# First attention chunks of a three-stage kernel: values pooled on TensorE, softmax by half tiles, reordered loads, and products of zeros

## The chip, the cores and the metric

The kernel runs on one core of a Trainium2 chip. The metric is device time in microseconds, the median of several runs. One execution was profiled; it has its own time and a span (first to last instruction).

## The reference

Three stages, one after the other, all in float32:

```
k_p, v_p = mean of k, v over groups of 8 rows                  # (4 batches, 8 heads, 576 rows, 64) -> 72 rows
attn = softmax(q @ k_p.T / 8) @ v_p                            # -> x: 2304 tokens x 512
x = (relu(x @ w_in) ** 2) @ w_out                              # 512 -> 2048 -> 512
e = argmax(x @ w_gate); g = its softmax probability            # 8 experts, capacity 576
out[i] = g[i] * (relu(x[i] @ w1[e]) @ w2[e])                   # 512 -> 1024 -> 512, if the expert has room
```

## The kernel before, in words

The 2304 tokens are nine chunks of 256 (`NCH`), a chunk two token tiles of up to 128 (`tiles_of_chunk`). Each chunk runs through attention, then through the dense layer in 16 slices of 128 hidden units (`g1`: the product `h`, relu, square, a split into a high and a low part, and the second product into `y`). Chunks 0 and 1 share the time in which the dense layer's weights arrive and are split, so their slices alternate; chunks 2 to 8 follow one by one, each with the next chunk's attention between its slices. Routing and the experts follow.

*Precision.* The large products run in float32r, a form with a shorter mantissa, one record of the trace a product. So every operand is split into a high and a low part, and a product is three: high by high, low by high, high by low. The products of attention (`qk` L429, the values L556) are plain float32. `conv` (L266) loads one of 32 dense weight tiles (128 x 512) and makes the two parts: `last` and `scale` on ScalarE, `sign` and `merge` on VectorE, `high` on ScalarE, `low` on VectorE (L307).

*Attention of one token tile.* `k_pool` (L328) sums groups of 8 columns of a head pair's keys on VectorE, `k_place` (L373) copies the sums into `kT` so that two heads of a pair share a product. `v_pool` (L347) sums the values likewise, in five blocks of 128 rows, and `v_zero` (L388) multiplies each block with masks into `vz` on GpSimd. `a_scores` (L418) loads a query tile, makes the scores of heads 0 to 3 and of heads 4 to 7 in two products each (the half-tiles `a` = 0 and 1), then the maximum, the subtraction, the exponential, the sum, its inverse, and the normalisation (`norm` L469, on GpSimd, or on VectorE for the tiles in `NORM_DVE`). In chunks 0 to 2 (`DVE_SOFTMAX`) the subtraction is one VectorE instruction for four heads and the exponential one on ScalarE; elsewhere ScalarE makes it head by head with the sum (L447). The sum, its inverse and the normalisation wait for all eight heads. `a_trans` (L511) transposes the probabilities in five blocks and ScalarE copies them out; `a_values` (L540) multiplies them with `vz` and splits the result into `xh` and `xl`, which the dense layer reads.

*What sets the order.* Every step is handed to a planner (`Steps`, L113) by `add(priority, engine, cost, function, reads, writes)`. It plays the program with costs in nanoseconds: at each turn it takes, over all engines, the step that can start first, by priority within an engine (lower is earlier), and emits it. Its clocks are only a plan; what it fixes is the order in each engine's queue, and the engines run their queues in order. It doubles the cost of TensorE's steps until TensorE has been busy for a while, and lengthens VectorE's steps marked `port` that meet a GpSimd step (`SHARE`). The constants ahead of the code (L62 to L82) are priorities: `CH0` and `CH1` place the attention of chunks 0 and 1, `Q0` their query loads, `V0_LOAD` and `CONV_LOAD` the loads of values and of weight tiles, `CONV_LEAD` and `CONV_AHEAD` how far ahead of its use a tile is split and loaded. All these loads are issued by one queue, SP's, in order of priority. `SQUARE_ACT` names the priorities between which chunks 0 and 1 are squared on ScalarE and not on VectorE; a slice's priority is twice its place in the order of slices.

Of the kernel before, what the change touches and what calls it, by code (L numbers as in the profile page):

```python
# [7 lines left out]
F32 = mybir.dt.float32  # L8
# [62 lines left out]
ATT2 = 16  # L71
# [12 lines left out]

def f(ap):
    return ap.bitcast(F32)
# [26 lines left out]
class Steps:  # L113
# [16 lines left out]

    def add(self, prio, eng, cost, fn, r=(), w=(), u=(), lat=0, port=False):
# [36 lines left out]
    def run(self):  # L168
# [6 lines left out]
        while any(todo.values()):  # L175
# [30 lines left out]
            if s.port:  # L206
                o = {"DVE": "POOL", "POOL": "DVE"}[e]
                if self.port[o] > t:
                    cost += min(cost, self.port[o] - t) * self.SHARE[e]
                self.port[e] = t + cost  # L210
# [7 lines left out]
def tile_kernel(ctx: ExitStack, tc: tile.TileContext, q, k, v, w_in, w_out, w_gate, w1, w2, cap, gate_rows, consts, out):  # L218
# [47 lines left out]
    def conv(i, prio, load_prio):  # L266
# [39 lines left out]
        def low():  # L306
            nc.vector.tensor_tensor(out=W[i][:, 1], in0=f(box["a"]), in1=f(W[i][:, 0]), op=ALU.subtract)  # L307

# [3 lines left out]
        add(prio, "ACT", 572, scale, w=(raw,))  # L312
        add(prio, "DVE", 340, sign, r=(raw,), w=(cv,), port=True)
        add(prio, "DVE", 605, merge, r=(raw,), w=(cv,), port=True)
        add(prio, "ACT", 525, high, r=(cv,), w=(("W", i, 0),), u=(whole,))
        add(prio, "DVE", 605, low, r=(cv, ("W", i, 0)), w=(("W", i, 1),), port=True)

# [10 lines left out]
    def k_pool(b, x, prio, load_prio, tag=None):  # L328

        buf, box = Buf("kvraw" if tag is None else tag), {}  # L330

        def load():
            box["raw"] = raw_tile(tag, f"kraw_{b}_{x}")
            nc.sync.dma_start(out=box["raw"], in_=k[b, x])

        def pool():
            nc.vector.tensor_reduce(
                out=kd[:, x], in_=box["raw"].rearrange("p (s r) -> p s r", r=POOL), axis=AX.X, op=ALU.add
            )

        add(load_prio, "SP", 960, load, w=(buf,), lat=2100)
        add(prio, "DVE", 663, pool, r=(buf, "ap"), w=(("kd", x),))

# [3 lines left out]
    def v_pool(b, i, prio, load_prio, tag=None):  # L347
# [20 lines left out]
        if ("v", b, i) in FOLD:  # L368
            add(prio, "POOL", 1300, fold, r=("ap",), w=(buf, ("v", i)))
        else:  # L370
            add(prio, "DVE", 603, pool, r=(buf, "ap"), w=(("v", i),))

    def k_place(b, prio):  # L373
# [44 lines left out]
    def a_scores(c, j, prio, qprio):  # L418
# [67 lines left out]
        for part in [tags] if c == 2 else [tags[:1], tags[1:]]:  # L486
            add(prio(2), "PE", 480 * len(part), lambda part=part: [qk(*x) for x in part],
                r=(qT, *(y for x in part for y in (("kT", 0, x[0]), ("kT", 1, x[0]), ("kT in", x[0]))), "ap", *after),
                w=[cells[x[0]] for x in part], u=us[part[0][0]])
        if c in DVE_SOFTMAX and (c, j) not in ACT_SOFTMAX:  # L490
            for a in range(2):
# [14 lines left out]
        if (c, j) in NORM_DVE:  # L506
            add(prio(4), "DVE", 663, lambda: norm(nc.vector), r=((mxb, 2),), w=((ex, 0), (ex, 1)), u=(mxb, ex), port=True)
        else:
            add(prio(4), "POOL", 1110, lambda: norm(nc.gpsimd), r=((mxb, 2),), w=((ex, 0), (ex, 1)), u=(mxb, ex))
# [620 lines left out]
    def wgb_load():  # L1130
# [7 lines left out]
        st["wgb"] = wgb  # L1138

    add(-100, "DVE", 600, start_up, w=[("kT", a, g) for a in range(2) for g in range(2)])  # L1140
    for x in range(NPAIR):
        k_pool(0, x, -90 + x, -99, f"W{27 + x}" if x < 2 else f"W{11 + x}")
        if x == 1:
            add(-98, "SP", 300, lambda: cst_load(0, C_TRI), w=("cst",), lat=2000)
# [3 lines left out]
    for i in range(5):  # L1148
        v_pool(0, i, V0_AT, V0_LOAD[i], f"W{22 + i}")
    for c, (at0, gap, slope) in enumerate((CH0, CH1)):  # L1150
# [5 lines left out]
        for j in range(2):  # L1156
            a_scores(c, j, lambda x, j=j: place0(x, j), Q0[c, j])
        if c == 0:
            v_zero(0, V0_AT + 1)
# [6 lines left out]
    add(2, "POOL", 100, late, w=("zt",))  # L1166
    add(4, "SP", 300, late_loads, w=("wg4", "capi"), lat=2000)
# [12 lines left out]
    for c in range(NCH):  # L1180
# [7 lines left out]
        if 2 <= c < NCH - 2:  # L1188
            for x in range(16):
                add(done + 1 + x, "DVE", 725, lambda c=c, x=x: logit(c, x % 2, x // 2), r=(lr[x % 2], "wgb", "wp"),  # L1190
                    w=(("lg", c, x),), u=(ysb[c], lgb[c]), port=True)
            late_routing.append((c, done + 18))
        for i in range(2):
            if c == BACK[i][0]:
                for t in range(2):
                    at, buf = place[c, 0] + BACK[i][1] + 8 * BACK[i][2] * t, Buf("kvraw")
                    add(at - 6, "SP", 760, lambda i=i, t=t: y_back(i, t), r=(("yd", i, t), "ap"), w=(buf,), lat=2000)
                    for x in range(8):
                        add(at + BACK[i][2] * x, "DVE", 725, lambda i=i, t=t, x=x: logit(i, t, x), r=(buf, "wgb", "wp", "ap"),
                            w=(("lg", i, 2 * x + t),), u=(lgb[i],), port=True)  # L1200
                late_routing.append((i, at + 8))
# [541 lines left out]
def _columns(q, k, v):  # L1743
# [6 lines left out]
    kt = k.reshape(B, NPAIR, P // D, S, D).transpose(0, 1, 2, 4, 3).reshape(B, NPAIR, P, S)  # L1750
    vt = v.reshape(B, NROW, POOL, D).transpose(0, 1, 3, 2).reshape(B, NROW, D * POOL)
    return np.concatenate(tiles), kt, vt

# [38 lines left out]
```

## Time and profile before

| | |
|---|---|
| median of 3 runs (lowest, highest) | 685.24 us (684.99, 685.41) |
| the profiled execution | 685.61 us, its span 683.9 us |
| TensorE busy | 659.2 us, 96% |
| VectorE, ScalarE, GpSimd busy | 421.9, 326.6, 186.8 us |
| keys and values of batch 0, queries of two chunks | 4 x 288 KB, 4 x 256 + 128 KB, 4 x 256 KB |
| dense weights | 32 x 512 KB |

How to read it: PE is TensorE, PEld its loading of the stationary operand, DVE VectorE, ACT ScalarE, POOL GpSimd, SP the engine that issues loads. A product in plain float32 leaves two records (passes), one in float32r or a transpose one. The length of one product holds its way through the pipeline, so products that follow each other overlap; the distance of their starts is what one costs. Idle time is put down to what ended it last.

### The profile page before, as it was taken

Reading aid. Unit: us, or ns where it says so; the run is one execution under the profiler, and the core shown is the slowest. Engines: PE = TensorE matmul, PEld = TensorE weight load, DVE = VectorE, ACT = ScalarE, POOL = GpSimd, SP = SyncE. Lnnn points to the kernel's source line nnn. Section 1 sums busy time; section 2 is a strip of 40 time slices with the busy share of each in tenths; the row PEclk is TensorE's granted clock in tenths of the full one; section 3 lists DMA queues with packets and bytes.
Section 4 is the critical chain, followed back from the end, with each engine's and each line's share of the span. In section 5 each row is a group of like instructions: output and inputs, shape, how many; then the busy total and the mean of one; then the engine's idle time right before and its main releaser. Section 6 shows DMA issues by size and latency. Waiting matters only on the chain. (4 is left out here: it accounts for less than half of the span.)

```text
span 683.9 us, 11883 instructions
## 1 busy us (share of the span) xinstructions
PE 659.2 (96%) x4211; PEld 593.4 (87%) x4212; DVE 421.9 (62%) x1123; ACT 326.6 (48%) x905; POOL 186.8 (27%) x221
## 2 busy tenths in 40 slices
PE   3799999999999999999999999999999999999996
PEld 2788899999899999989899899998997979889985
DVE  6999997221288999374288647445354556464352
ACT  5898884344353344255344344343432555454352
POOL 1334543223234233234233132242202211301110
PEclk9899999999999999999999999999999999999999
DMA  8998904110222320011010000062005764655110
GB/s 308 395 365 306 296 31 128 58 47 17 92 78 59 93 78 9 1 41 30 1 48 17 2 32 1 2 222 88 1 33 161 246 220 135 209 163 174 48 60 3
DMA packets 40970, 73.46 MB, mean 107 GB/s; under 512 B 8449, under 2 KB 17921, under 8 KB 40768
## 3 DMA queue, kind: packets, MB, share of 16 engines
q1 hardware_dynamic: 38496, 64.89, 28.0%
q0 software_dynamic: 2400, 7.66, 3.4%
q8 instruction: 37, 0.61, 0.4%
q14 instruction: 37, 0.30, 0.1%
HBM read 59.63 MB, written 13.12 MB: 106 GB/s over the span
## 5 line engine op out<-in xcount | busy, mean ns | idle before, releaser
L628 PE MATMUL h<-xh,W 128*128 128x256 f32 x1152 | 213.4, 284 | 0.2
L648 POOL TENSOR_TENSOR gl<-r,gh 128x256 fp32r<-128x256 f32 x144 | 116.9, 812 | 285.1 <-ACT gh L644 184.9
L628 PEld LDWEIGHTS h<-xh,W 128*128 128x128 f32 x1152 | 184.0, 189 | 10.2 <-ACT xh L562 0.3
L661 PE MATMUL y<-W,gh 128*128 128x512 f32 x576 | 185.1, 402 | 0.3 <-DVE W L307 0.3
L628 PE MATMUL h<-xl,W 128*128 128x256 f32 x576 | 161.8, 281 | 0.8 <-DVE xl L566 0.8
L640 DVE SCALAR_TENSOR_TENSOR r<-h,r 128x256 f32<-128x256 f32 x141 | 59.0, 419 | 100.4 <-ACT r L633 100.1
L633 ACT ACTIVATE r<-h 128x256 f32<-128x256 f32 x144 | 55.1, 382 | 123.8 <-PE h L628 104.9
L661 PE MATMUL y<-W,gl 128*128 128x512 f32 x288 | 113.6, 394 | 0.0
L661 PEld LDWEIGHTS y<-W,gh 128*128 128x128 f32 x576 | 99.4, 189 | 15.7 <-DVE W L307 0.6
L628 PEld LDWEIGHTS h<-xl,W 128*128 128x128 f32 x576 | 108.9, 189 | 1.1 <-DVE xl L566 1.0
L644 ACT CAST gh<-r 128x256 fp32r<-128x256 f32 x144 | 58.5, 406 | 77.4 <-DVE r L640 77.0
L1356 PE MATMUL hp<-yh,W 128*128 128x256 f32 (+1 forms) x384 | 74.5, 291 | 0.9 <-issue 0.9
L718 DVE SCALAR_TENSOR_TENSOR junk<-ysb,wgb 128x512 bf16<-128x512 f32 x80 | 68.5, 856 | 1.4
L661 PEld LDWEIGHTS y<-W,gl 128*128 128x128 f32 x288 | 54.1, 188 | 13.1 <-POOL gl L648 0.3
L1356 PEld LDWEIGHTS hp<-yh,W 128*128 128x128 f32 x384 | 61.1, 188 | 1.6 <-issue 1.0
L1325 PE MATMUL po<-W,xh_e 128*128 128x512 f32 x192 | 61.3, 401 | 0.0
L1356 PE MATMUL hp<-yl,W 128*128 128x256 f32 (+1 forms) x192 | 55.7, 290 | 0.0
L250 DVE TENSOR_TENSOR W<-stg,W 128x512 fp32r<-128x512 f32 x64 | 42.3, 689 | 12.4 <-ACT W L249 11.2
L1325 PEld LDWEIGHTS po<-W,xh_e 128*128 128x128 f32 x192 | 34.7, 188 | 6.8
L1362 DVE SCALAR_TENSOR_TENSOR xl_e<-hp,xh_e 128x256 fp32r<-128x256 f32 x48 | 20.2, 422 | 31.4 <-ACT xh_e L1361 31.2
L1314 POOL DMA_INDIRECT out_dram<-ysb,sidx x12 | 11.9, 995 | 98.3 <-ACT ysb L1303 84.7
L471 POOL TENSOR_TENSOR ex<-ex,sm 128x576 f32<-128x576 f32 (+1 forms) x19 | 25.4, 1338 | 47.7 <-DVE sm L467 28.5
(207 smaller groups left out, 908.8 us busy)
## 6 DMA issues: line engine op xcount, KB each, us to landing
stg<-in_moe_w_dram SPq DMA_DIRECT2D x40, 512.0 KB, 5.0
raw<-in_moe_w_in_dram SPq DMA_DIRECT2D x16, 512.0 KB, 7.5
raw<-in_moe_w_out_dram SPq DMA_DIRECT2D x16, 512.0 KB, 7.3
kraw<-in_k_dram SPq DMA_DIRECT2D x16, 288.0 KB, 3.0
out_dram<-zt SPq DMA_DIRECT2D x18, 256.0 KB, 3.6
y_dram<-ysb SPq DMA_DIRECT2D x18, 256.0 KB, 2.1
qT<-in_q_dram SPq DMA_DIRECT2D x16, 256.0 KB, 3.0
vraw<-in_v_dram SPq DMA_DIRECT2D x16, 256.0 KB, 3.6
```

Source lines behind the costliest of these rows:

```text
L250: eng.tensor_tensor(out=lo, in0=src, in1=f(hi), op=ALU.subtract)
L471: eng.tensor_tensor(out=ex[:n], in0=ex[:n], in1=sm[:n].unsqueeze(2).to_broadcast([n, H, SP]), op=ALU.mult)
L628: nc.tensor.matmul(ps, wt[kk][:, l, o:o + P], r[:, kk, :], start=(n == 0), stop=(n == 3 * KD - 1))
L633: nc.scalar.activation(out=box["r"], in_=box["ps"], func=AF.Relu)
L640: nc.vector.scalar_tensor_tensor(out=r, in0=box["ps"], scalar=0.0, in1=r, op0=ALU.max, op1=ALU.mult)
L644: nc.scalar.copy(out=box["gh"], in_=box["r"])
L648: nc.gpsimd.tensor_tensor(out=box["gl"], in0=box["r"], in1=f(box["gh"]), op=ALU.subtract)
L661: nc.tensor.matmul(st["y", c][t], l[:, ts], r, start=(ff == 0 and n == 0), stop=(ff == NF - 1 and n == 2))
L718: nc.vector.scalar_tensor_tensor(out=junk, in0=st["yb", c, t] if c < 2 else st["ysb", c][t], scalar=1.0, in1=st["wgb"][:, e], op0=ALU.mult ...
L1325: nc.tensor.matmul(ps, l, r, start=(fi == 0 and x == 0), stop=(fi == 7 and x == 2))
L1356: nc.tensor.matmul(ps, ww[:, l, o], r[:, kk, 0:n2], start=(kk == 0 and x == 0), stop=(kk == KD - 1 and x == 2))
L1362: nc.vector.scalar_tensor_tensor(out=lo, in0=p_, scalar=0.0, in1=f(h), op0=ALU.max, op1=ALU.subtract)
```

## The change

1. *Products of zeros.* `warm_up(m)` issues m products of the zero tile `zt` by itself (128 x 128, plain float32) into a PSUM tile that nobody reads. 26 of them stand first in TensorE's queue, 13 behind the first half-tile's scores of chunk 0, 2 behind the first half-tile's scores of its second token tile. The zero tile is set at the start.
2. *Values of batch 0 pooled on TensorE.* Eight products with the identity, one for each of the 8 rows of a group, are added up in PSUM (`v_pool0`); VectorE multiplies the result with the masks into `vz`. The rows are laid out by the host so that five blocks take three loads.
3. *Softmax of chunk 0 by halves of four heads* (`HALVES`): sum, inverse and normalisation are made for each half-tile. For the halves in `ACT_HALF` (both of the first token tile; its entries for chunk 1 have no effect) ScalarE makes the exponential head by head with its sum. The second token tile's halves are normalised on VectorE, the first one's on GpSimd.
4. *Order of loads.* The second key tile, the first, the first query tile, the other two key tiles, the second query tile; then values, constants and weight tiles, the fourth weight tile behind the third query tile.
5. *Other engines.* The third key tile of batch 0 is pooled on GpSimd by three additions (`KFOLD`); the low parts of weight tiles 0, 2 and 3 are made on GpSimd (`LOW_POOL`); the squares of ten more slices go to ScalarE.
6. *Constants and planner costs.* Due times, the costs of shared ports, the loads of batch 3, and the last chunk's softmax (`DVE_SOFTMAX`, 8).

```diff
-V0_LOAD = (-70, -70, -70, -70, -70)
-CONV_LOAD = (-96, -96, -95, -95)
-CONV0 = (-20, -19, -18, -17)
+V0_LOAD = (-96.0, -96.4, -94.4)
+K0_LOAD = (-98.6, -99, -98.4, -98.4)
+CST1 = -96.2
+WARM = 26
+CONV_LOAD = (-96, -96, -95, -56.5)
+CONV0 = (-37.8, -19, -18, -17)
...
-CONV_LEAD = 3
-CONV_AHEAD = 6
+CONV_LEAD = 2.4
+CONV_AHEAD = 1.9
...
-CH1 = (0, 2, 0.5)
-V0_AT = -45
-Q0 = {(0, 0): -98.5, (0, 1): -97, (1, 0): -50, (1, 1): -50}
+CH1 = (0, 2, 0.42)
+V0_AT = -45.9
+Q0 = {(0, 0): -98.5, (0, 1): -98, (1, 0): -83.5, (1, 1): -50}
...
-SQUARE_ACT = (-99, 6)
-NORM_DVE = ((0, 1),)
-KV_AT = {1: (20, 1.0), 2: (66, 3), 3: (130, 3)}
-DVE_SOFTMAX = (0, 1, 2)
+SQUARE_ACT = (-99, 26.0)
+NORM_DVE = ((0, 1, 0), (0, 1, 1))
+HALVES = (0,)
+FILL = ((0, 0, 0, 13), (0, 1, 0, 2))
+KFOLD = (2,)
+ACT_HALF = ((1, 1, 1), (0, 0, 1), (1, 0, 1), (0, 0, 0), (1, 1, 0))
+LOW_POOL = (3, 0, 2)
+KV_AT = {1: (20, 1.0), 2: (66, 3), 3: (128.9, 3.93)}
+DVE_SOFTMAX = (0, 1, 2, 8)
...
-    SHARE = {"DVE": 0.7, "POOL": 0.5}
+    SHARE = {"DVE": 1.0, "POOL": 0.4}
...
+        def fold():
+            y = box["raw"].rearrange("p (s r) -> p s r", r=POOL)
+            for w in (4, 2):
+                nc.gpsimd.tensor_tensor(out=y[:, :, 0:w], in0=y[:, :, 0:w], in1=y[:, :, w:2 * w], op=ALU.add)
+            nc.gpsimd.tensor_tensor(out=kd[:, x], in0=y[:, :, 0], in1=y[:, :, 1], op=ALU.add)
...
+    def v_pool0(i, prio, buf):
...
+            for r in range(POOL):
+                nc.tensor.matmul(
+                    o, ident[ps], st["vraw", i][:, :, r], start=(r == 0), stop=(r == POOL - 1)
+                )
...
+            nc.vector.tensor_tensor(out=o, in0=box["ps"][ps].unsqueeze(1).to_broadcast([n, w, D]), in1=m, op=ALU.mult)
...
+        add(prio, "PE", 860, pool, r=(buf, "cst"), w=(h,))
+        add(prio, "DVE", 65 + 69 * w, place, r=(h, "cst", "ap"), w=(("vz", i),))
...
+            for y in FILL:
+                if y[:3] == (c, j, part[0][0]):
+                    add(prio(2), "PE", 108 * y[3], lambda m=y[3]: warm_up(m), r=(cells[y[2]],), w=(warm,), u=us[y[2]])
+        if c in HALVES:
+            for a in range(2):
...
+                add(prio(3), "DVE", 368, lambda a=a: top(a), r=w, w=((mxb, a),), u=(*u, mxb, ex))
+                if (c, j, a) in ACT_HALF:
+                    for h in range(4 * a, 4 * a + 4):
+                        add(prio(3), "ACT", 300, lambda h=h: exp(h), r=w, w=((ex, a), (mxb, a)), u=(*u, mxb, ex))
+                else:
+                    add(prio(3), "DVE", 365, lambda a=a: less(a), r=(*w, (mxb, a)), w=((ex, a),), u=(*u, mxb, ex))
+                    add(prio(3), "ACT", 335, lambda a=a: exp4(a), w=((ex, a),), u=(ex,))
+                    add(prio(4), "DVE", 365, total, r=((ex, a),), w=((mxb, a),), u=(mxb, ex))
+                add(prio(4), "DVE", 220, inverse, w=((mxb, a),), u=(mxb,))
+                if (c, j, a) in NORM_DVE:
+                    add(prio(4), "DVE", 365, lambda norm2=norm2: norm2(nc.vector), r=((mxb, a),), w=((ex, a),), u=(mxb, ex), port=1)
+                else:
+                    add(prio(4), "POOL", 590, lambda norm2=norm2: norm2(nc.gpsimd), r=((mxb, a),), w=((ex, a),), u=(mxb, ex))
+            return
...
+    def warm_up(m):
+        if "warm" not in st:
+            st["warm"] = pg.tile([P, P], F32, tag="g", name="warm")
+        for _ in range(m):
+            nc.tensor.matmul(st["warm"], st["zt"], st["zt"], start=True, stop=True)
...
+    add(-100, "POOL", 300, late, w=("zt",))
+    add(-100, "PE", 108 * WARM, lambda: warm_up(WARM), r=("zt",), w=(warm,))
```

## Rows read from the trace of the kernel before

**Rows 1.** Busy time by stretch: window, length, each engine, PEclk, DMA share, GB/s.

```profile
8.21:26.81 18.60, 12.38 (x59) 11.29 (x59) 17.07 (x34) 13.86 (x31) 4.79 (x6) 0.82 1.04 375
...
26.81:34.46 7.65, 6.65 (x51) 5.97 (x50) 7.65 (x18) 7.35 (x20) 1.85 (x2) 1.00 1.04 410
...
34.46:40.00 5.54, 4.62 (x25) 3.42 (x24) 5.54 (x9) 4.01 (x11) 2.61 (x3) 1.00 1.03 411
...
40.00:640.00 600.00, 597.64 (x3855) 539.19 (x3854) 368.43 (x1016) 282.61 (x809) 172.71 (x200) 1.00 0.29 96
```

**Rows 2.** Who waited for whom, TensorE, whole run: us in total, times, longest.

```profile
PE ata L520 <- DVE ex L471: 3.3, 1, 3.3
...
PE ata L520 <- POOL ex L471: 2.9, 1, 2.9
...
PE sc L432 <- DVE xl L566: 0.5, 1, 0.5
...
PE y L661 <- DVE W L307: 0.3, 1, 0.3
```

**Rows 3.** Busy time by stretch, finer; PEclk is the granted clock.

```profile
19.59:22.30 2.71, 2.71 (x11) 2.62 (x12) 2.65 (x6) 1.33 (x3) 1.52 (x3) 0.50 1.07 395
...
22.30:26.81 4.51, 4.51 (x28) 4.12 (x27) 4.51 (x11) 4.33 (x9) 0.00 (x0) 1.00 1.06 390
```

**Rows 4.** TensorE's timeline: start us, length us, line, operation, tiles, passes.

```profile
8.21 4.08 PE L432 MATMUL sc<-kT,qT 128*128 128x144 f32 x16 [8.21 <-DVE kd L337]
...
25.43 1.63 PE L432 MATMUL sc<-kT,qT 128*128 128x144 f32 x12
...
34.46 0.60 PE L520 MATMUL ata<-cst,ex 128*128 128x128 f32 x4
...
34.90 0.27 PE L525 MATMUL atb<-cst,ex 128*128 128x128 f32 x1
...
39.69 3.72 PE L556 MATMUL av<-aT,vz 128*128 128x256 f32 x16 [0.59 <-ACT aT L530]
...
46.05 0.40 PE L628 MATMUL h<-xh,W 128*128 128x256 f32 x2
...
46.40 0.40 PE L628 MATMUL h<-xh,W 128*128 128x256 f32 x2
```

**Rows 5.** Groups of TensorE instructions by form, whole run: count, busy us, mean ns.

```profile
L556 PE MATMUL av<-aT,vz 128*128 128x128 f32 x32 | 3.9, 275 | 0.0
...
L556 PE MATMUL av<-aT,vz 128*128 128x64 f32 x32 | 3.8, 271 | 0.0
...
L748 PE MATMUL lp<-wg,ytl 128*128 128x8 f32 x32 | 3.7, 251 | 0.0
```

**Rows 6.** Timeline of the first 8 us.

```profile
0.92 0.20 POOL L1117 MEMSET zt<- 128x128 f32 x1
...
6.11 0.75 DVE L337 TENSOR_REDUCE kd<-kraw 128x72 f32<-128x576 f32 x1 [0.93 <-DMA kraw<-in_k_dram]
...
7.44 0.75 DVE L337 TENSOR_REDUCE kd<-kraw 128x72 f32<-128x576 f32 x1 [0.58 <-DMA kraw<-in_k_dram]
```

**Rows 7.** Groups by line, whole run: count, busy us, mean ns, idle before.

```profile
L640 DVE SCALAR_TENSOR_TENSOR r<-h,r 128x256 f32<-128x256 f32 x141 | 59.0, 419 | 100.4 <-ACT r L633 100.1
...
L447 ACT ACTIVATE ex<-sc,mx 128x72 f32<-128x72 f32 (+1 forms) x104 | 32.2, 322 | 7.1 <-DVE mx L442 7.1
...
L447 ACT ACTIVATION_READ_ACCUMULATOR ex<-sc,mx 128x1 f32 (+1 forms) x104 | 21.5, 206 | 0.0
...
L359 DVE TENSOR_REDUCE pv<-vraw 128x64 f32<-128x512 f32 (+1 forms) x20 | 13.4, 674 | 6.1 <-DMA vraw<-in_v_dram 6.1
```

**Rows 8.** Timeline around 76 us: VectorE's low part, TensorE's products.

```profile
76.01 0.69 DVE L307 TENSOR_TENSOR W<-cv,W 128x512 fp32r<-128x512 f32 x1
...
76.51 0.28 PE L628 MATMUL h<-xh,W 128*128 128x256 f32 x1
```

**Rows 9.** Timeline: GpSimd and VectorE side by side, and a merge alone.

```profile
13.98 1.14 POOL L471 TENSOR_TENSOR ex<-ex,sm 128x576 f32<-128x576 f32 x1 [12.86 <-DVE sm L467]
...
14.13 1.54 DVE L298 SCALAR_TENSOR_TENSOR cv<-raw,cv 128x512 int32<-128x512 int32 x1
...
24.79 0.68 DVE L298 SCALAR_TENSOR_TENSOR cv<-raw,cv 128x512 int32<-128x512 int32 x1
```

More of the change, by code (lines that the diff above doesn't have):

```diff
@@ L129, in __init__, with add @@
         self.steps, self.writer, self.readers = [], {}, {}
-    def add(self, prio, eng, cost, fn, r=(), w=(), u=(), lat=0, port=False):
+    def add(self, prio, eng, cost, fn, r=(), w=(), u=(), lat=0, port=0):
         s = Step(prio, eng, cost, fn, lat, port or eng == "POOL")
@@ L208, in run @@
                 if self.port[o] > t:
-                    cost += min(cost, self.port[o] - t) * self.SHARE[e]
+                    cost += min(cost * s.port, self.port[o] - t) * self.SHARE[e]
                 self.port[e] = t + cost
@@ L306, in low @@
         def low():
-            nc.vector.tensor_tensor(out=W[i][:, 1], in0=f(box["a"]), in1=f(W[i][:, 0]), op=ALU.subtract)
+            eng = nc.gpsimd if i in LOW_POOL else nc.vector
+            eng.tensor_tensor(out=W[i][:, 1], in0=f(box["a"]), in1=f(W[i][:, 0]), op=ALU.subtract)
         whole = Buf(f"W{i}")
@@ L312, in conv @@
         add(prio, "ACT", 572, scale, w=(raw,))
-        add(prio, "DVE", 340, sign, r=(raw,), w=(cv,), port=True)
-        add(prio, "DVE", 605, merge, r=(raw,), w=(cv,), port=True)
+        add(prio, "DVE", 340, sign, r=(raw,), w=(cv,), port=2)
+        add(prio, "DVE", 605, merge, r=(raw,), w=(cv,), port=1)
         add(prio, "ACT", 525, high, r=(cv,), w=(("W", i, 0),), u=(whole,))
-        add(prio, "DVE", 605, low, r=(cv, ("W", i, 0)), w=(("W", i, 1),), port=True)
+        add(prio, *(("POOL", 1050) if i in LOW_POOL else ("DVE", 605)), low, r=(cv, ("W", i, 0)), w=(("W", i, 1),), port=1)
     kT = ap.tile([P, NROW], F32, tag="kT", name="kT")
@@ L341, in k_pool @@
         add(load_prio, "SP", 960, load, w=(buf,), lat=2100)
-        add(prio, "DVE", 663, pool, r=(buf, "ap"), w=(("kd", x),))
+        def fold():
[3 more added lines that the diff above has]
+            nc.gpsimd.tensor_tensor(out=kd[:, x], in0=y[:, :, 0], in1=y[:, :, 1], op=ALU.add)
+        if b == 0 and x in KFOLD:
+            add(prio, "POOL", 1450, fold, r=("ap",), w=(buf, ("kd", x)))
+        else:
+            add(prio, "DVE", 663, pool, r=(buf, "ap"), w=(("kd", x),))
     def v_rows(i):
@@ L371, in v_pool, with v_load0, load, pool @@
             add(prio, "DVE", 603, pool, r=(buf, "ap"), w=(("v", i),))
+    def v_load0(i, load_prio, tag):
+        buf = Buf(tag)
+        def load():
+            m = 2 if i < 4 else 1
+            t = cpool.tile([P, 2, POOL * D], F32, tag=tag, name=f"vraw_0_{i}")
+            if m == 2:
+                src = v[0, 0:4 * P].rearrange("(p i) d -> p i d", i=4)[:, i:i + 2]
+                nc.sync.dma_start(out=t, in_=src)
+            else:
+                nc.sync.dma_start(out=t[v_rows(4), 0], in_=v[0, 4 * P:NROW])
+            for x in range(m):
+                st["vraw", i + x] = t[v_rows(i + x), x].rearrange("p (d r) -> p d r", r=POOL)
+        add(load_prio, "SP", 1300 if i < 4 else 430, load, w=(buf,), lat=2100)
+        return buf
+    def v_pool0(i, prio, buf):
+        ps, n, h, box = v_rows(i), min(P, NROW - i * P), Buf("h"), {}
+        c0, w = max(0, 2 * i - 1), 2 if i in (0, 4) else 4
+        def pool():
+            o = box["ps"] = pp.tile([P, D], F32, tag="h", name=f"pv0_{i}", bufs=2)
+            for r in range(POOL):
+                nc.tensor.matmul(
+                    o, ident[ps], st["vraw", i][:, :, r], start=(r == 0), stop=(r == POOL - 1)
+                )
+        def place():
+            o = vz[ps, c0:c0 + w // 2].rearrange("p s r d -> p (s r) d")
+            m = cst[ps, C_VM + 2 * c0:C_VM + 2 * c0 + w].unsqueeze(2).to_broadcast([n, w, D])
+            nc.vector.tensor_tensor(out=o, in0=box["ps"][ps].unsqueeze(1).to_broadcast([n, w, D]), in1=m, op=ALU.mult)
+        add(prio, "PE", 860, pool, r=(buf, "cst"), w=(h,))
+        add(prio, "DVE", 65 + 69 * w, place, r=(h, "cst", "ap"), w=(("vz", i),))
     def k_place(b, prio):
@@ L506, in a_scores @@
         if (c, j) in NORM_DVE:
[L507 removed]
+            add(prio(4), "DVE", 663, lambda: norm(nc.vector), r=((mxb, 2),), w=((ex, 0), (ex, 1)), u=(mxb, ex), port=1)
         else:
@@ L1147, in tile_kernel @@
     k_place(0, -60)
-    for i in range(5):
-        v_pool(0, i, V0_AT, V0_LOAD[i], f"W{22 + i}")
+    for i in (0, 2, 4):
+        buf = v_load0(i, V0_LOAD[i // 2], f"W{22 + i}")
+        for x in range(i, min(i + 2, 5)):
+            v_pool0(x, V0_AT + 0.1 * x, buf)
     for c, (at0, gap, slope) in enumerate((CH0, CH1)):
```

28 lines of the change are left out of this document (19 added, 9 removed).

## The prediction

> **What bounds the kernel now.** I read the stretches first. From 40 to 640 us TensorE is busy 597.64 of 600.00 us [rows 1]: there the time is the sum of TensorE's work, and a faster helper engine buys nothing. All that can be won lies ahead of 40 us. TensorE does nothing until 8.21 us, is busy 12.38 of the next 18.60, then 6.65 of 7.65 and 4.62 of 5.54 [rows 1]. The list of TensorE's waits names the holes: 2.9 and 3.3 us for the normalised softmax of the two token tiles, later 0.5 us for the second chunk's low part and 0.3 us for a converted weight tile [rows 2]; one of 0.59 for the transposed probabilities stands in the row at 39.69 [rows 4]. The granted clock is at its lower level (0.50, 1.2 GHz) from 19.59 to 22.30 us, when TensorE had just come out of its long waits, and full (1.00, 2.4 GHz) afterwards [rows 3]. At the very start no row shows the clock, but the instructions do: 16 score passes took 4.08 us at 8.21 and 12 took 1.63 us at 25.43, so 255 against 136 ns each [rows 4].
>
> So I make the sum on TensorE, between its first score product (8.21 us) and the end of the fourth group of first-layer products (34.46 us, where transposes start, [rows 4]). At full clock that stretch holds 16 score passes x 0.136 = 2.2, 10 transposes x 0.11 (four from 34.46 to 34.90) = 1.1, 16 value passes x 0.2325 (3.72/16, [rows 4]) = 3.7, the second chunk's 16 score passes 2.2, and 48 first-layer products x 0.1175 (three from 46.05 to 46.40, [rows 4]) = 5.6, where they took 7.65: 14.8 us of work in 26.25 us. At most 11.4 us can be won there, 0.9 more before 40 us [rows 1], and 0.5 after it.
>
> **The change, part by part.** *Zero products at the start.* 26 calls of 128 by 128 in plain float32. The eight score calls ahead of 12.3 us left 16 passes [rows 4], so a call is two passes: 52. They start when the zero tile is set, about 1.1 us (its memset ends there, [rows 6]). A slow pass is 128/144 of the slow score pass, 0.227. After the restart at 19.59 the clock was full 2.7 us later [rows 3]; at 8.21 all 4.08 us of scores ran slow [rows 4]. With a rise 4.1 us after 1.1, 18 passes are slow and 34 x 0.116 (below) follow: the last ends at 9.1; with 2.7 us, at 8.4. I take 8.7. The price per pass is bounded from above by 0.136 (the score row) and from below by 0.110 (the transposes).
>
> *Queries between the keys.* The third load lands near 6.1 (the third key reduction starts there, [rows 6]); with the first query there, the first half's scores could start at about 6.1 instead of 8.21. But TensorE's queue is in order and the zero products stand ahead: they start at 8.7. Half a microsecond is lost, none gained; what is gained is the clock (2.2 against 4.1 us for the scores), and it is counted in the 14.8.
>
> *Zero products between the scores.* 13 calls behind the first half, 2 behind the third: 30 passes x 0.116 = 3.5 us. Queued behind the 13 are the remaining three half-tiles of scores, and behind these VectorE's maxima. The second half's keys are ready at about 9.6 (third key by GpSimd, fourth, now the fifth load, by VectorE up to about 8.9, as an estimate half a microsecond behind its 7.44 + 0.75 now, [rows 6], then the copy that places it), the 13 calls end at 12.3: they overrun the hole that they fill by 2.7 us.
>
> *Values pooled on TensorE.* 5 blocks x 8 calls x 2 passes = 80 passes of 64 columns. The price is the crux. By columns alone a 64-column pass would be half of a transposed 128 columns, 55 ns, 4.4 us in all. But float32 passes here do not get cheaper with fewer columns: 32 of 128 columns took 3.9 us, 32 of 64 took 3.8, 32 of 8 columns took 3.7 [rows 5], that is 0.122, 0.119, 0.116. I take 0.116: 9.3 us (a block of 16 passes 1.86 us, where the planner's cost is 0.86). The nearest row decides, and the form is the same.
>
> The Trainium skill ("TensorE: Matmul & The Clock Gate", section "Back-to-back issue gap") gives 64 columns and fewer about 60 cycles when a product is looked at by itself; by that estimate (25 ns, or 50 if float32 doubles it) the 80 passes would cost 2 to 4 us and the sum below would end faster than before. That is R1's pooled block. The 8-column row contradicts it; the measurement decides.
>
> The five reductions leave VectorE (5 x 0.674 = 3.4 us, [rows 7]), the masked copies move from GpSimd to VectorE (five; no row shows them there, between nothing and the 3.4 us that they replace). All of that lies beside TensorE's longer work and is worth nothing. *Softmax by halves:* the first tile's exponentials go per head to ScalarE (8 x 0.322, or 0.53 with the read of the sum, [rows 7]), VectorE loses two subtractions and a sum and gains reciprocals (no row for a half; I take a wash). It lets a tile's first half be normalised earlier, but transposes wait for both halves. *Moved to other engines:* one key reduction (0.75 us) and the low parts of weight tiles 0, 2, 3 to GpSimd, ten squares (0.42 us on VectorE, [rows 7]) from VectorE to ScalarE. ScalarE is at 7.35 of 7.65 us in that stretch [rows 1]; cover: TensorE's lag gives it 2 us. *Loads:* values (1.15 MB, 3.1 us at the 375 GB/s of [rows 1]) go ahead of the first weight tiles, the fourth weight tile behind a query; weights land about 3 us later, which a TensorE that needs them only after 30 us does not feel. *New costs and due times* reorder everything later, and the last chunk's softmax moves to VectorE: cost 0, covered by the 600 us at 597.64, of which they could take back at most 0.5; if that cover fails, the price is a hole of 0.3 to 0.9 like those in [rows 2].
>
> *Sum.* Start 8.7; work 14.8 + 3.5 + 9.3 = 27.6; end at 36.3 if TensorE never waits, against 34.46: +1.8. Not all waits go: last transposes to copy to values (0.6 us as at 39.69), last pooled block to masked copy to second half of values (0.5, an estimate from the 0.6), and starts and ends of streams. I take +1.3 (bounds 0.5 and 2.5). Given back later: with the helpers ahead, the 0.9 us before 40 us and part of 0.5, together 1.1 (bounds 0 and 1.4). So +2.0 us on the profiled execution's 685.61 (span 683.9): 687.6. That execution is 0.37 above the median of the three runs, so **687.2**. With the pass at 0.110 and the best bounds the sum is -0.3 us, with 0.122 and the worst +5.3.
>
> **Rivals.** *R1, the passes cost what the planner's numbers say* (0.108 a zero call, 0.86 a pooled block): the zero products end at 6.1, then 14.8 + 1.6 + 4.3 = 20.7, end at 26.8 plus 1.3, 6.4 us earlier than 34.46; then VectorE (7.65 of 7.65) and ScalarE bind, each of which must deliver weight tiles earlier too: the twentieth tile is ready at 76.7 when its products start at 76.51 [rows 8], so there is no lead to spend. I take 2.4 back: -4, 681.2. For it: the fillers fit the holes by these costs. Against: [rows 5]. If only the zero calls are cheap, the gain is about 2 (683.3), counted here.
>
> *R2, no difference:* pass at 0.110 (8.8 + 3.3), waits 0.5, 1.4 given back: 8.5 + 26.9 + 0.5 = 35.9, +1.4 - 1.4 = 0: 685.2. For it: the holes are really there to be filled. Against: they are long only where dependent work stands.
>
> *R3, worse: GpSimd holds VectorE up.* A merge took 1.54 us beside a GpSimd product of 1.14 instead of 0.68 [rows 9], +0.86. Three low parts, one key fold and two half normalisations make six such chances, 5.2 us against 2.8 us taken off VectorE (3 x 0.69 by the low part in [rows 8], and 0.75). It decides once VectorE is later than TensorE by the first group of products: 2.4 us more, 689.6. Against: in the same stretch GpSimd loses its masked copies. The Trainium skill ("SBUF — State Buffer", section "Who interferes with whom") calls this an exclusive lock between GpSimd and a VectorE instruction with two SBUF inputs; [rows 9] agree.
>
> **How the numbers follow.** Chances: forecast 0.44, with its own range 685.7 to 689.0; R1 0.31; R2 0.16; R3 0.09. About 0.2% (1.37 us) is what a measurement can tell: faster is below 683.87, slower above 686.61. Faster: R1 0.29 and 0.03 of R2, 0.32. Within: 0.11 of the forecast, 0.12 of R2, 0.02 of R1, 0.25. Slower: 0.33 + 0.09 + 0.01, 0.43. The range leaves out the better part of R1 (0.12) and the far end of R3 and the sum (0.06): 681.0 to 690.0.
>
> **What would show it.** Right: two records per zero call, the last zero product ending near 8.7; pooled passes 0.11 to 0.12 apart; TensorE nearly without waits from 8.7 on and the first first-layer product after 29 us (26.81 now). Wrong: pooled blocks under 1 us, the first scores at about 6.1, the first first-layer product ahead of 25 us; or VectorE, not TensorE, still without a hole at 20 us. That the lower clock vanishes between 15 and 22 us is expected under every case but would fail if the products of zeros did not raise it; then the stretch is slower still.

## The result, and the profile after

The changed kernel takes 689.61 us (median of five runs, 688.86 to 689.89), the kernel before beside it 685.41 us: a ratio of 1.0059, 95% interval 1.0044 to 1.0073. It is slower by 4.2 us where the forecast said 2.0, that is slower as said and by twice as much. The profiled execution took 689.89 us with a span of 688.1 (before: 685.61 and 683.9), so the spans differ by the same 4.2. In the experiments below a time is the median of all runs, and the ratio leaves out runs more than 1.5% above the kernel's fastest.

The page's busy times, after: engine, us, share of the span, instructions.

```profile
PE 676.4 (98%) x4373; PEld 611.3 (89%) x4374; DVE 418.0 (61%) x1120; ACT 327.1 (48%) x899; POOL 188.9 (27%) x223
```

The shortest account stands in that line. TensorE was busy 659.2 us before: it now does 17.2 us more, and stands still 11.7 us of the span instead of 24.7. What was gained in waits, 13.0, was bought with more work than it was worth.

The stretches of TensorE's work after (window, length, each engine's busy time, granted clock, DMA share, GB/s), to be laid beside [rows 1]:

```profile
9.69:31.30 21.61, 21.61 (x171) 20.89 (x169) 15.01 (x38) 13.55 (x39) 3.30 (x4) 1.00 1.04 386
31.30:34.46 3.16, 1.70 (x13) 1.28 (x11) 3.16 (x6) 3.10 (x8) 1.83 (x2) 1.00 1.03 414
34.46:40.00 5.54, 5.34 (x43) 5.13 (x43) 5.53 (x16) 5.54 (x17) 3.23 (x4) 1.00 0.16 66
40.00:640.00 600.00, 596.84 (x3846) 538.05 (x3847) 372.68 (x1017) 285.19 (x800) 173.47 (x201) 1.00 0.30 99
```

From the first score product to the first first-layer product there is not one hole on TensorE and no low clock, where [rows 1] had 12.38 of 18.60 us and [rows 3] a clock of 0.50. VectorE has become the engine with gaps (15.01 of 21.61). But then TensorE, now late and dense, meets helpers that are not ready: 1.70 of 3.16 us.

TensorE's timeline after (start, length, line, operation, tiles, passes, the wait before it), which answers to [rows 4]; the second part is the first-layer products that wait.

```profile
1.04 8.82 PE L1212 MATMUL warm<-zt 128*128 128x128 f32 x52 [1.04 <-POOL zt L1206]
9.69 0.66 PE L488 MATMUL sc<-kT,qT 128*128 128x144 f32 x4
10.18 3.06 PE L1212 MATMUL warm<-zt 128*128 128x128 f32 x26
13.08 0.66 PE L488 MATMUL sc<-kT,qT 128*128 128x144 f32 x4
...
14.02 1.15 PE L488 MATMUL sc<-kT,qT 128*128 128x144 f32 x8
15.00 5.88 PE L417 MATMUL pv<-vraw,cst 128*128 128x64 f32 x48
20.70 0.62 PE L609 MATMUL ata<-cst,ex 128*128 128x128 f32 x4
...
21.27 2.06 PE L417 MATMUL pv<-vraw,cst 128*128 128x64 f32 x16
23.15 0.62 PE L609 MATMUL ata<-cst,ex 128*128 128x128 f32 x4
...
23.81 2.14 PE L417 MATMUL pv<-vraw,cst 64*128 64x64 f32 x16
25.87 1.25 PE L488 MATMUL sc<-kT,qT 128*128 128x144 f32 x8
26.96 3.62 PE L645 MATMUL av<-aT,vz 128*128 128x256 f32 x16
30.41 1.14 PE L488 MATMUL sc<-kT,qT 128*128 128x144 f32 x8
31.30 0.49 PE L717 MATMUL h<-xh,W 128*128 128x256 f32 x2
...
33.15 0.39 PE L717 MATMUL h<-xl,W 128*128 128x256 f32 x1 [0.66 <-DVE xl L655]
...
34.61 0.38 PE L717 MATMUL h<-xh,W 128*128 128x256 f32 x1 [0.96 <-POOL W L316]
```

By the distance of starts, the pooled values took 5.70 + 1.88 + 2.06 = 9.64 us for 80 passes, the fill between the scores 2.90 + 0.44. The first first-layer product starts at 31.30 us (26.81 before). Where the 4.2 us arise, by the starts in the two traces: +4.5 at the first first-layer product, +5.3 at the 48th (39.67 against 34.34; 0.5 of it are one tile's transposes, which now come before it), +5.3 at the last of all 1728 (501.99 against 496.65), and 1.1 come back in the experts' part behind it.

The list of TensorE's waits after (total us, times, longest). The waits of the first and the third line go away when the low parts leave GpSimd (low_dve, below); the others stand where the forecast expected the helper engines to be ahead:

```profile
PE h L717 <- POOL W L316: 1.0, 1, 1.0
PE y L750 <- DVE W L316: 0.8, 1, 0.8
PE h L717 <- DVE xl L655: 0.7, 1, 0.7
PE y L750 <- POOL gl L737: 0.5, 1, 0.5
PE ata L609 <- POOL ex L527: 0.5, 1, 0.5
```

And GpSimd's low part beside VectorE's merge, from the two engines' timelines (compare [rows 9]): the merge took 1.76 us, so `xl`, queued behind it, started at 32.42 while TensorE waited.

```profile
30.67 1.28 POOL L316 TENSOR_TENSOR W<-cv,W 128x512 fp32r<-128x512 f32 x1 [5.93 <-ACT W L312]
33.28 1.28 POOL L316 TENSOR_TENSOR W<-cv,W 128x512 fp32r<-128x512 f32 x1 [1.33 <-ACT W L312]
```
```profile
30.74 1.76 DVE L306 SCALAR_TENSOR_TENSOR cv<-raw,cv 128x512 int32<-128x512 int32 x1
32.42 0.68 DVE L655 TENSOR_TENSOR xl<-av,xh 128x512 fp32r<-128x512 f32 x1
```

The last reading is of the start. VectorE's and ScalarE's timelines after, around the first scores:

```profile
10.38 0.46 DVE L498 TENSOR_REDUCE mx<-sc 128x4 f32<-128x288 f32 x1 [5.27 <-PE sc L488]
10.76 0.74 DVE L346 TENSOR_REDUCE kd<-kraw 128x72 f32<-128x576 f32 x1
```
```profile
11.78 0.31 ACT L436 ACTIVATE kT<-kd 64x144 f32<-64x144 f32 x1
...
12.42 0.32 ACT L436 ACTIVATE kT<-kd 64x144 f32<-64x144 f32 x1
```

The fourth key reduction stands behind the first maximum in VectorE's queue, and the copies that place the second half's keys stand among and behind the first exponentials on ScalarE. VectorE waited 5.27 us for the scores with that reduction queued behind the wait. So the second half's keys are not ready at 9.6 us: they follow the first scores by about three microseconds, whenever these start. The zero products at the start delay both halves.

### The profile page after: what moved, and what is told of

The parts are those of the page before. It is cut to its first block, busy times and chain, and to the rows that moved or that the text cites. A ratio compares the mean times of both kernels' runs of the same rounds, so it can differ in the third digit from the quotient of the medians.

```text
span 688.1 us, 12205 instructions
## 1 busy us (share of the span) xinstructions
PE 676.4 (98%) x4373; PEld 611.3 (89%) x4374; DVE 418.0 (61%) x1120; ACT 327.1 (48%) x899; POOL 188.9 (27%) x223
## 5 line engine op out<-in xcount | busy, mean ns | idle before, releaser
L729 DVE SCALAR_TENSOR_TENSOR r<-h,r 128x256 f32<-128x256 f32 x131 | 55.1, 421 | 107.4 <-ACT r L722 107.1
L1421 PE MATMUL po<-W,xl_e 128*128 128x512 f32 x96 | 37.8, 394 | 0.0
```

The lines of the kernel that those rows point to most:

```text
L729: nc.vector.scalar_tensor_tensor(out=r, in0=box["ps"], scalar=0.0, in1=r, op0=ALU.max, op1=ALU.mult)
L1421: nc.tensor.matmul(ps, l, r, start=(fi == 0 and x == 0), stop=(fi == 7 and x == 2))
```

## The experiments

Each kernel is the changed one with the edit shown, unless said otherwise; the ratio is to the kernel before on the same chip. "First product" is the start of the first first-layer product (26.81 us before, 31.30 after), "the 48th" and "the last" likewise (34.34 and 39.67; 496.65 and 501.99).

**no_zeros.** All zero products leave the program; the order of the rest stays.

```diff
-add(prio(2), "PE", 108 * y[3], lambda m=y[3]: warm_up(m), ...)
+add(prio(2), "PE", 108 * y[3], lambda: None, ...)
-add(-100, "PE", 108 * WARM, lambda: warm_up(WARM), ...)
+add(-100, "PE", 108 * WARM, lambda: None, ...)
```

> The changed kernel (689.6) without its products of zeros; every other instruction in the same order on each engine. Theory, the sum on TensorE: the first scores start when keys and query are there, near 6.5 instead of 9.69 us; the second half's scores then wait for their keys until about 10; the pooled blocks start near 12 instead of 15.0, but with the slow clock for their first passes, which gives back up to 1.6. So 1.5 to 3 us faster than the changed kernel: 686.6 to 688.1. Rival, the zero products pay by holding the clock up: the pooled blocks and transposes run slow to the end of attention, 2 to 4 us slower than the changed kernel: 691.6 to 693.6.

Measured: 688.84 us (686.16 to 697.39), ratio 1.0026 (1.0011 to 1.0041). The scores start at 6.17 and the pooled values at 12.03 instead of 15.00; the first product comes at 30.66, 0.6 us earlier. Of that lead 2.3 us were lost again to the clock: the first 48 pooled passes were busy 6.54 us instead of 5.88 (0.7), and the 16 score and 16 value passes behind the pooled ones, from 23.56 on, took 7.1 us instead of 5.4 (1.7). The windows view:

```profile
12.03:23.80 11.77, 11.77 (x93) 11.47 (x93) 7.75 (x21) 6.77 (x20) 2.00 (x2) 1.00 1.06 373
23.80:27.20 3.40, 3.40 (x13) 3.04 (x13) 2.59 (x7) 2.51 (x5) 0.00 (x0) 0.50 1.02 395
```

The granted clock fell to 0.50 in the middle of unbroken work. So all zero products together buy a little less than they cost (1.0026 without them, 1.0059 with them); the rival's 691.6 and more, by which the clock is worth 2 to 4 us net, was not reached.

**no_fill.** Only the 15 calls between the scores leave.

> The changed kernel without the 15 calls of zeros between the scores; the 26 at the start stay, all else in the same order. Their 30 passes take 3.5 us of TensorE. Theory: but the second half's scores can't start before the key copies of ScalarE (12.42 to 12.74 in the changed kernel, behind the exponentials), so the pooled blocks come forward from 15.0 to about 13.9 only: 1.1 us faster, 688.5. If the passes cost their full length, 3.5 us: 686.1. Rival, they hold the clock: slower than 689.6.

Measured: 693.77 us, ratio 1.0081 (1.0049 to 1.0114), but the runs lay between 688.8 and 701.9, so the time decides nothing. The trace does: the pooled values start 4.18 us behind the first scores instead of 5.31, so the fill cost 1.1 us and not its own 3.3. TensorE stood 1.95 us waiting for `kT`, which came at 11.76 with the first scores at 8.66: 3.1 behind them. The first product comes at 29.14 and the last at 499.92, each about 2.1 earlier than in the changed kernel; in the experts' part, which took 188.0 us instead of 186.1, nearly all of that went again.

**low_dve.** `LOW_POOL = ()`: the low parts of weight tiles 0, 2 and 3 go back to VectorE.

> The changed kernel with the low parts of weight tiles 0, 2 and 3 on VectorE again (LOW_POOL empty; the planner orders anew). Theory of the sum on TensorE: only the waits inside the first group of first-layer products (0.66 for the low part of x, 0.96 for the low part of a weight tile from GpSimd) can go: 1.0 to 1.6 us faster, 688.0 to 688.6. The rival of GpSimd holding VectorE up: 2.4 faster, 687.2, with the merge of 1.76 us at 30.74 down to 0.68. If neither matters: 689.6.

Measured: 687.59 us, ratio 1.0024 (1.0010 to 1.0039), 2.0 less than the changed kernel. The waits of 0.66 and 0.96 are gone: from the first product to the 48th it took 6.9 us, the changed kernel 7.9 without the transposes that it has in between. VectorE's merges around the first products (starts 28.16 and 29.69) take 0.68 us. Of the new waits one stands out in its list:

```profile
PE y L750 <- DVE W L316: 1.5, 1, 1.5
```

The last product starts 3.2 us earlier than in the changed kernel, of which 0.9 is an earlier end of the zero products at the start (scores at 8.78). So three low parts on GpSimd, with the order that the planner makes of them, cost about 2 us where the forecast's sum put nothing; R3 had 2.4 for all its six chances.

**v_dve.** The values are pooled on VectorE and masked on GpSimd as before the change; the rest of the change stays.

```diff
-    for i in (0, 2, 4):
-        buf = v_load0(i, V0_LOAD[i // 2], f"W{22 + i}")
...
+    for i in range(5):
+        v_pool(0, i, V0_AT, V0_LOAD[i // 2], f"W{22 + i}")
```

> The changed kernel with the values of batch 0 pooled on VectorE and masked on GpSimd as before; the loads keep the new priorities, the planner orders anew. 80 passes, 10.1 us in the changed kernel's trace, leave TensorE. Theory: the values' product then waits for the softmax and comes at 22.5 to 24 instead of 26.96: 3 to 4.5 us faster, 685.1 to 686.6. Rival, TensorE isn't the bound there: VectorE and GpSimd take 3.4 and 3.6 us more and the holes come back whole, 0 to 1.5 faster: 688.1 to 689.6.

Measured: 689.45 us, ratio 1.0048 (1.0032 to 1.0063). The rival held. The first product comes at 27.90, 3.4 us earlier, but the last one at 502.05. What took the lead back, from its list of waits and its windows:

```profile
PE ata L609 <- POOL ex L563: 3.9, 2, 3.7
PE y L750 <- POOL gl L737: 1.7, 1, 1.7
PE h L717 <- DVE xl L655: 1.2, 2, 1.0
```
```profile
73.75:77.16 3.41, 3.41 (x14) 3.03 (x14) 3.41 (x5) 2.41 (x6) 1.84 (x2) 0.50 1.06 375
```

The long wait for the normalised softmax is back (compare [rows 2]), then the helpers are late among the first weight tiles, and a wait of 1.7 us is followed by a stretch at half the clock. (An earlier one, 19.13 to 22.55 us, follows the wait for the softmax.) That the values' pooling alone made the helpers late is not shown, since the planner ordered all engines anew.

**fill_double.** 26 and 4 calls between the scores in the place of 13 and 2, at half the planner's cost, so in the same order.

> The changed kernel with twice the zero products between the scores (26 and 4 calls for 13 and 2); the planner's cost for them is kept, so all else is in the same order. Theory, the sum on TensorE: 30 more passes of 0.118 lie on the path at their full length, the first first-layer product comes 3.5 us later and the time is 3.5 us above the changed kernel's, 693.1 against 689.6. Rival, they lie in holes: 689.6 to 690.5.

Measured: 693.47 us, ratio 1.0117 (1.0100 to 1.0134): 3.86 more for 30 more passes; 52 of them took

```profile
9.14 5.97 PE L1212 MATMUL warm<-zt 128*128 128x128 f32 x52
```

by the distance to the next scores 5.81, 0.112 each, which makes 3.35 for 30. By the trace the first product comes 24.96 us behind the first scores, in the changed kernel 21.61: again 3.35. Once the hole is filled, a further zero product is paid in full; for the 0.5 beyond that, its list of waits has 0.9 more before 140 us (for `gl` 0.9 against 0.5, for `xl` 0.7 against 0.2).

**v_16bit.** The pooled values are summed from the upper 16 bits of each float (so less exactly), in one pass a call in the place of two.

```diff
-o, ident[ps], st["vraw", i][:, :, r], ...
+o, half(ident[ps]), half(st["vflat", i])[:, r::POOL], ...
```

> The changed kernel with the pooled values made from the upper 16 bits of values and identity (bfloat16 operands, so the values are cut to 8 bits of mantissa): one pass a call instead of two, 40 for 80, the same steps in the same order. A test of the price of the pooled passes. Theory: the 10.1 us of the pooled blocks fall to 4.7 or less; the values' product then waits for the second tile's softmax and comes 2.5 to 3.7 us earlier than 26.96; 686.0 to 687.1. Rival, the helpers bind: the first first-layer product comes earlier, but waits for weight tiles give it back; 688.6 to 689.6.

Measured: 685.46 us, ratio 1.0000 (0.9987 to 1.0013), so 4.15 less than the changed kernel. 24 passes took 2.99 us to the next start (18.04), 0.125 each: half the passes at about the same price each, for a step of 32 bytes in both forms. All 40 took 4.94 us, 4.7 less than the 80.

```profile
15.05 3.17 PE L419 MATMUL pv<-vraw,cst 128*128 128x64 bf16 x24
```

Of these, 4.15 reach the end, without any work put back on VectorE, although the clock read 0.50 from 30.82 to 34.23 us. So the pooled passes lie on the path at full length, as the forecast's sum had them. That v_dve gained nothing is then the doing of VectorE and GpSimd and of the clock behind their waits.

**true_costs.** The order that the planner makes when it is told what the passes cost (1960 ns a block, 235 and 225 a zero call).

> The changed kernel, planned with the costs that the trace shows: 235 for a zero call (225 at the start), 1960 for a pooled block. No instruction is added or removed, only the order may move. Theory: TensorE's work is the same, so at most its waits of 1.6 us inside the first product groups go: 688.0 to 689.6. Rival, the fault is the order that wrong costs made: 2 us faster or more, 687.6 or less.

Measured: 695.01 us, ratio 1.0137 (1.0120 to 1.0154). Both theories missed. Transposes moved ahead of pooled blocks, TensorE waited 1.8 us for the normalised softmax, and this followed (windows):

```profile
20.58:37.64 17.06, 16.36 (x66) 15.11 (x67) 10.46 (x27) 10.15 (x21) 3.20 (x3) 0.50 1.04 408
37.64:41.00 3.36, 3.36 (x25) 3.18 (x23) 2.52 (x5) 3.08 (x7) 0.00 (x0) 1.00 1.03 415
```

17 us at half the clock, in which TensorE was busy but for the 0.7 us that were left of the wait. The first product came at 40.95 instead of 31.30, the last at 506.75 instead of 501.99: TensorE, that late, waited for no helper in the dense layer, and half of the lag came back. Two rows from within the slow stretch will be used below; the products behind them start at 28.70 and 29.54:

```profile
21.97 6.92 PE L417 MATMUL pv<-vraw,cst 128*128 128x64 f32 x32
28.70 1.04 PE L609 MATMUL ata<-cst,ex 128*128 128x128 f32 x4
```

**mended.** 12 zero products at the start, none between the scores, low parts on VectorE, and the true costs.

> The changed kernel with 12 calls of zeros at the start (24 passes, over near 6.4 us), none between the scores, the low parts on VectorE and the true costs; values stay on TensorE. Theory: scores start at about 6.5 instead of 9.69; 14.8 us of work and 10.1 of pooled blocks with 2 us of waits end the fourth group of first-layer products near 33.5 instead of 39.7: 5 us faster than the changed kernel, 684.6, about 1 below the kernel before. Rival, the supply of weight tiles binds as soon as TensorE is early: 686 to 688.

Measured: 692.57 us, ratio 1.0101 (1.0061 to 1.0141), but the runs lay between 687.0 and 696.7. In the profiled execution (687.95 us) the last first-layer product starts at 495.52, 6.5 us ahead of the changed kernel and 1.1 ahead of before. The lead was lost in the experts' part:

```profile
PE po L1421 <- issue: 2.5, 1, 2.5
...
PE yTp L1012 <- issue: 1.4, 1, 1.4
```

The profile names nothing that they waited for. Behind the wait of 2.5 us the granted clock was 0.50 from 526.7 to 530.1 us. The five executions of 687.0 to 689.7 us had a mean granted clock of 0.991 to 0.996, the five of 695.5 to 696.7 one of 0.979 to 0.982, so more time at the lower clock goes with the longer time; where in the kernel, no trace shows.

**pairs.** The four blocks of values that share two loads are pooled two at a time (`m` = 2), 128 columns a pass.

```diff
-o = box["ps"] = pp.tile([P, D], ...)
+o = box["ps"] = pp.tile([P, m, D], ...)
-o, ident[ps], st["vraw", i][:, :, r], ...
+o, ident[ps], st["vpair", i][:, :, r::POOL], ...
```

> The four blocks of pooled values that share two loads are pooled two at a time: a pass has 128 columns, 32 passes in the place of 64, the last block stays at 16. Exact, like the changed kernel. Theory (a pass costs 0.12 us whatever its columns): 48 passes, 5.8 to 5.9 us in the place of 10.1, first first-layer product near 27.1 (31.3 in the changed kernel), and since that lead was kept whole when the passes were halved by 16-bit values: 685.0 to 686.0. Rival A (price by columns): 128-column passes cost 0.24, nothing is won, 689.6. Rival B (as with values pooled on VectorE, the helper engines and the clock take the lead back): first product near 27, but 688 to 689.6.

Measured: 690.74 us, ratio 1.0077 (1.0064 to 1.0091). Rival A held. 32 passes of 128 columns were busy 7.6 us by the groups by form, the 64 of 64 columns 7.9 us in the changed kernel, while a pass of a zero product, 128 columns too, took half (26 in 2.90 us).

```profile
L416 PE MATMUL pv<-vraw,cst 128*128 128x128 f32 x32 | 7.6, 412 | 0.0
```

By starts 7.44 us for 32, 0.2325 a pass, against 0.1115 for the zero products and 0.116 to 0.122 for the contiguous forms of [rows 5]. The pooled passes read every eighth float; the zero products and those forms read neighbours. So at this step a column costs 1.8 ns. 64 of them cost 0.117, which is also what few neighbouring columns cost: at 64 columns the two prices meet, and pairing saves nothing.

**pairs_low.** Pairs, with `LOW_POOL = ()`.

> Pairs, and the low parts of weight tiles 0, 2 and 3 on VectorE again. Theory: the waits of 0.66 and 0.96 us among the first products go, as they did alone (2 us less than the changed kernel there, of which about 0.9 was the start of the clock): 1.0 to 1.6 below pairs, 683.7 to 684.7. Rival: with TensorE 4 us earlier VectorE is the bound among the first weight tiles (a wait of 1.5 us for it stood in that run already), and its three low parts cost 2 us: no less than pairs, 685 to 687.

Measured: 690.96 us, ratio 1.0075 (1.0062 to 1.0088): no less than pairs. Without the two waits the first 48 products took 7.1 us (8.3 in pairs without the transposes in between), but in the profiled execution the clock read 0.56 from 26.16 to 29.50 us, which put the first product at 33.27.

**pairs_lean.** As pairs_low, with `FILL = ()`.

> Pairs, low parts on VectorE, and the 15 zero products between the scores left away (the 26 at the start stay). Theory: the fill cost 1.1 us on the path where it was taken out alone: 682.7 to 683.7. Rival: the second half's keys set the start of the scores in any case and the helpers the rest: as the kernel with pairs and low parts, 684 to 685.

Measured: 692.06 us (689.26 to 692.75), ratio 1.0094 (1.0080 to 1.0108). In the trace the first product comes at 30.02 and the last at 499.18, 2.8 ahead of the changed kernel; the time is worse all the same. 3.2 us of waits in the experts' part that the changed kernel has for 1.1 stand in the profiled execution, which was its fastest run; of the others there is no trace, and why the time is worse than the dense layer says stays open (mean granted clock 0.998 in that run, 0.993 to 0.997 in the others).

**pairs_w12.** As pairs_lean, with `WARM = 12`.

> As the one before, with 12 zero products at the start in the place of 26. Theory: the zero products end near 6.6, the first half's scores start 2 us earlier, but the second half's still wait for its keys until about 12, so nothing is won: within 0.7 us of the kernel with 26. Rival: the earlier scores pass on to the softmax and the first transposes: 1 to 2 us less, 681 to 682.5. Other rival: TensorE's clock falls in the longer hole, as it did with 12 and without fill before: 685 or more.

Measured: 682.97 us (682.10 to 684.65), ratio 0.9966 (0.9953 to 0.9979): faster than both kernels, and its first rival held. TensorE's timeline and its stretches:

```profile
1.04 5.49 PE L1213 MATMUL warm<-zt 128*128 128x128 f32 x24 [1.04 <-POOL zt L1207]
6.32 0.85 PE L489 MATMUL sc<-kT,qT 128*128 128x144 f32 x4
8.15 0.76 PE L489 MATMUL sc<-kT,qT 128*128 128x144 f32 x4 [0.98 <-DMA qT<-in_q_dram]
9.52 1.73 PE L489 MATMUL sc<-kT,qT 128*128 128x144 f32 x8 [0.61 <-ACT kT L437]
11.05 3.92 PE L416 MATMUL pv<-vraw,cst 128*128 128x128 f32 x16
...
15.35 3.89 PE L416 MATMUL pv<-vraw,cst 128*128 128x128 f32 x16
...
27.21 0.49 PE L718 MATMUL h<-xh,W 128*128 128x256 f32 x2
```
```profile
10.13:13.54 3.41, 3.41 (x17) 3.41 (x16) 3.02 (x11) 2.66 (x12) 0.67 (x1) 0.50 1.03 398
...
27.21:34.46 7.25, 6.55 (x53) 6.03 (x52) 6.74 (x16) 7.25 (x21) 3.17 (x3) 1.00 1.04 415
```

The scores start 2.59 us earlier than in pairs_lean (8.91), `kT` of the second half comes 2.5 earlier (9.52 against 12.01), the first product 2.8 (27.21) and the last 4.1 (495.12); the spans differ by 5.7 (681.8 and 687.5), the last 1.6 of it in the experts' part; the medians differ by 9.1, for which one trace of each can't account. Fourteen zero products fewer, and one transpose group that the planner moved ahead of a pooled pair, are the whole difference in TensorE's queue up to the first product.

The other rival's fall of the clock came too: behind the two waits it was 0.50 from 10.13 to 13.54 us. (In mended, the kernel with 12 and without fill that this rival points to, it stayed at 1.00 from the first scores to the first product.) Yet only the last scores were slower for it. The pooled passes took 0.234 us each from 11.05 to 14.79, mostly at the lower clock, and 0.232 from 15.35 to 19.06 at the full one.

That the pairing adds anything is unlikely by its price. The same kernel without it was not run; the nearest is mended, which has no pairs and other planner costs. Its dense layer ends at 495.52, 0.4 behind, and its loss lies behind that.

## Why the prediction was right in sign and half in size

**The work sum held.** From the first score product to the first first-layer product the forecast has 22.0 us of work (scores 4.4, transposes 1.1, values 3.7, fill 3.5, pooled 9.3); TensorE took 21.61 and never waited. fill_double and v_16bit show the two new terms on the path at their price. R1, whose two prices were the planner's, is out: a pooled block took 1.9 us. That the total fits so well is in part luck: scores and value products were priced by their length (0.136, 0.2325), while their starts here are 0.123 and 0.216 apart, so 0.7 too much there made up for 0.3 too little in the pooled blocks.

**The price was right, but its rule is half of the story.** The forecast took 0.116 a pass because [rows 5] show few columns costing as much as many. 64 columns cost 0.119 and their 128-column version 0.2325 (pairs): at a step of eight floats columns cost too. The two rules meet at 64 columns and the full clock, so the sum did not notice. At the lower clock they part. In true_costs 32 pooled passes of 64 columns took 6.73 us (0.210 each), and four transposes of 128 columns beside them 0.84 (0.21 each): there a pass has its price whatever its columns, as the forecast had it. In pairs_w12 the passes of 128 columns cost the same at both clocks: there the step sets the price. Each pass also has a load of its stationary operand of its own (PEld busy 20.89 of 21.61 us in the stretch above); whether that load is the price of a pass with few columns was not tried. The Trainium skill ("SBUF — State Buffer", section "Door 1: The DMA port swizzle (why `[64,N]` ≈ `[32,N]`)") says that reads that jump to a new 16-byte line each time pay for it, and that a step of up to four floats is free; the runs agree for a step of eight and 128 columns (0.2325 against 0.1115), and smaller steps were not run.

**The zero products end later.** Forecast 8.7, scores at 9.69: +1.0. Their passes start 0.21 us apart up to 6.7 us and 0.11 from 6.9 on, so the full clock, which the forecast had at 3.8 to 5.2, came later. In the other kernels that start with the same 52 passes the scores began between 8.65 and 9.74, so part of it is this execution. The text then said "half a microsecond is lost, none gained" and "the second half's keys are ready at about 9.6", as if these came on their own. That is the failed step of the start: they come 3.1 to 3.8 us behind the first scores (no_fill, no_zeros), because their reduction and their copies are queued behind the maximum and the exponentials. So the 13 calls overran their hole by some 0.3 us instead of 2.7 (all 15 cost 1.1, no_fill), and the calls ahead of the scores, costed at 0.5, were the dear ones: 14 fewer bring the first product 2.8 us forward (pairs_w12 against pairs_lean).

**More waits than the 1.3 allowed, and nothing given back.** Among and behind the first products TensorE waited 3.7 us (the list's 1.0, 0.8, 0.7, 0.5 and 0.5, and 0.2 more), within which 1.6 are R3's mechanism: the low part late on GpSimd and the merge held to 1.76 beside it. Without the low parts on GpSimd the time is 2.0 less (low_dve). R3 was given 0.09 as a case of its own; it was there in part, beside the forecast. The 1.1 to be given back in the dense layer did not come: the lag is 5.3 at the 48th product and at the last. At the 48th the sum had a lag of 3.1 (1.8 and 1.3); the 2.2 between are 1.0 for the start, 1.1 for the waits within these products (2.4 us above their 5.6 of work, where 1.3 was allowed) and 0.5 for the transposes that moved ahead, less 0.4 of work. An amount like the 1.1 came back behind the dense layer, in the experts' part (before 187.25 us from the last first-layer product to the end, after 186.11), and not by the helpers' lead. That part took between 186.1 and 190.7 us in the traces of these kernels, so as far as the forecast goes this 1.1 is luck.

**What was said to show it** was there: two records a zero call, passes about 0.12 apart, no wait from the first scores on, the first first-layer product after 29 us, no low clock between 15 and 22 us.

## What to carry to other kernels

Work put ahead of the first real product pays only until the data lands: look up what is queued behind that product on the other engines before calling its delay free. Take a product's price from a row with the same step in memory, not only the same type and number of columns. And when one engine is relieved, ask for each helper whether it could have delivered earlier: v_dve won 3.4 us on TensorE up to the first product and lost all of it in waits for GpSimd and VectorE and at a lower clock. The kernel that beat both keeps the values on TensorE (in pairs), with the low parts where they were, no fill and 12 zero products at the start (pairs_w12).

## What the runs showed of the hardware

The granted clock fell to its lower level although TensorE had no hole: in no_zeros at 23.80 us, after 11.77 us of 11.77 busy, and in pairs_low at 26.58, after 2.49 of 2.49 (a wait of 0.57 stands before that). In true_costs it fell in a wait of 1.57 us and then stayed down for 17.06 us of nearly unbroken products. Pooled passes and transposes had gone before in all three; whether they bring it about was not tried. In the changed kernel the same passes kept the full clock.

A pass in plain float32 reading every eighth element took 0.2325 us for 128 columns, one reading neighbours 0.1115; and in 16-bit form, with the same 32 bytes from element to element, 64 columns took 0.125. The lower clock made transposes (0.21 us apart in true_costs against 0.115 in the changed kernel) and pooled passes of 64 columns (0.210 against 0.119) nearly twice as long, but left those of 128 columns at that step as they were (0.234 against 0.232, pairs_w12).
